# One kernel, its 1410 steps issued in another order

## The chip, the cores and the metric

The kernel runs on one core of a Trainium2 chip. The metric is the device time of one launch in microseconds (us). TensorE (PE in the profile) multiplies, VectorE (DVE), ScalarE (ACT) and GpSimd (POOL) work element by element, and SyncE (SP) issues every DMA from one queue that is worked off in order.

## The reference

The inputs are r, k, v, w of 4 batches, 8 heads, 768 tokens and 48 channels, and u of 8 heads and 48 channels. A recurrence with decay runs over the tokens, and its output goes through a feed-forward block (FFN):

```python
for t in range(S):
    cur = np.einsum('bhd,bhe->bhde', u[None] * kt, vt)
    y[:, :, t] = np.einsum('bhd,bhde->bhe', rt, state + cur)
    state = wt[:, :, :, None] * state + np.einsum('bhd,bhe->bhde', kt, vt)
...
xt = x.transpose(0, 2, 1)              # x: (4, 768, 384), the heads side by side
h = xt @ U @ V                         # mixes the tokens, rank 32
u = x + h.transpose(0, 2, 1)
ch = np.maximum(u @ w_ch1, 0.0) @ w_ch2    # 384 -> 1536 -> 384
return (u + ch).astype(np.float32)
```

## The kernel before

**Tiles.** The tokens of a batch are cut into 6 chunks of 128, so there are 24 chunks, numbered 0 to 23. Each chunk is a row of steps; a step is one small function that issues a few instructions on one engine. A step's name is a word for its work and the number of its chunk or block:

- LW, LRK, LKR, LV (SP, lines 400 to 417): loads of w, of r and k transposed, of k and r by rows, and of v. v has two buffers, so LV of a later chunk waits until an earlier chunk has been read. LRAW (L268) loads a piece of a weight, OUT (L925) stores a part of the output.
- F, R, Q (DVE, L435, L444, L449): running products of w, forward and as reciprocal. T (L172 on DVE, L170 on ACT) copies the total decay.
- PR, RP, KS, RK, RU (lines 517, 455, 459, 481, 484): elementwise products, each on POOL or DVE. DV, RED, SEL, SEL2 make a diagonal.
- AM (PE, L572) makes the scores of a chunk, CP (DVE, L576) masks them, YA and YZ (PE, L636 to L663) make the output from scores and from the state, DS (PE, L583) makes the update of the state out of k and v, ZA and ZM (L608, L617 or L619) apply it.
- KD (DVE, L560), KW and KB (SP, L377 and L383) turn k for some chunks by a transpose of blocks, a store to DRAM and four loads; KB waits for KW's data. KT and KN do it by PE. XE, XT, XN, XD do the same for the output x.
- GA, G4, SELM, GS, GSL, HP, UADD, UH, UL: the mixing by U and V. UH and UL split u into a high and a low part (ULP and UHP in the first block). UL of all three thirds must be done before the first UP of a block.

**FFN.** Each batch has 2 blocks of 384 tokens, block 0.0 to block 3.1. UP b.blk.f (PE, L867, 9 matmuls of 384 columns) makes one of 12 hidden slices, HH (ACT L874 or DVE L876) and HL (DVE L880) split it into high and low, DN b.blk.ct.part (PE, L902, 9 matmuls) adds three slices into one of three outputs, and O (DVE, L921) adds the result to x. The weights are split into high and low once: LRAW, then AB, E, SG, JN, HI, SUB per piece, w1 in 12 pieces for UP, w2 in 12 for DN. E, SG, HI, SUB, like T, HH, XE, XN, RP, KS, RK, RU, UH, UL, have an alternative engine.

**What sets the order.** Nothing is scheduled at run time. All steps of all engines stand in one list that is written out by hand as the string `ORDER`: three characters a step, two for its number and one, `how`, whose lowest bit chooses the alternative engine and whose rest is a count of warming matmuls to issue before it (`warm(s.lead)`; two counts are one bf16 matmul of 512 columns, whose result is not used). `plan` turns the string into the list:

```python
i, how = DIGITS.index(ORDER[n]) * 64 + DIGITS.index(ORDER[n + 1]), DIGITS.index(ORDER[n + 2])
...
if how % 2:
    s.eng = s.alt
s.lead = how // 2
```

An engine works its own steps in the order of the list. Between engines only the waits count that the data and the buffers demand. The list also says which buffer a step gets, since a buffer that was freed earlier is given out first.

Of the kernel before, what the change touches and what calls it, by code (L numbers as in the profile page):

```python
# [60 lines left out]

DIGITS = "0123456789ABCDEFGHIJKLMNOPQRSTUVWXYZabcdefghijklmnopqrstuvwxyz+-"
ORDER = (
    "2u02v02z02-03003502w03K03L00502+136+3113213703803A83N02y03P03913m03V00U03Q03S00003n03M04D03C03D03B03EM3W0070"
# [4 lines left out]
    "4z05B07i04+17g03l05J00u05007k05100K00a01304A05K08301807h00C04B00P01205240v05R05L05307r05M05N07l05S01411h00L0"
    "7n15O07m15Y07s00Q15P07t08608805Q00M08D08908C00O05T05U05V07u05W01505X08B07v07x07w08f07z01U07o07y05Z05a15c0871"  # L70
    "5d00y01X05e05f05h09O08E05i08A01600R08J05j05m05b01707-05k05g01A18L05l01Y16d07j15n00S00T18008W08V01905q01Z00z1"
    "0x08F08Y06e08x08+05o08g08a01B11i08h05r08d05t00+05p06C05s08508b01j08y01M01O06600-01018G05u08K08c16D08H08101k1"
    "5v01C09406E08I08i01P11l06301D06706I07+08208M00b09001E01m06J11N06406508j00d02702800e12901Q08N08Q08R08S00i0910"
    "6809308n01n00c01o00k18l06K06002A08Z10l18X08k01R10f08m01a01S12B06902000j00m00g06106206F00h00n06A06B02C09211b0"
    "8O00o15w06G01q15z01c01v08o09X09B02E01r01d01p01s08P11t02201u01e06f18s08t06H05x18p02L05+15-01f01g01w01x05y02S0"
    "9D06h01y12306i09N02g09C01z02D02G02101+02Z02F02H06L06M0CL01-12M02402508T06j16l06g02U12I02J08u02i12619502K12T0"
    "2V02W02b09q02c12N12O02P02Q08e06m06n02X16N06O06R06S06T02R02Y16U02n06P06k16o12p12a02d06X09Q06Q02j19Y06V08q09V1"
    "8z06s06W0CK08U02h09619707506t16u02e02o02f02q17607707K02k09S09Z02l02m02r06Y0980CU02s07B09a09z08-1CN07L09W09b0"
# [1066 lines left out]
```

## Time and profile before

| | |
|---|---|
| median of three runs | 427.59 us (424.26, 427.63, 427.59) |
| the profiled execution | 424.35 us, its span 422.5 us |
| PE busy | 411.8 us, 97% of the span |
| DVE busy | 279.2 us, 66% |
| ACT, POOL busy | 161.2 us, 38%; 129.4 us, 31% |
| mean granted TensorE clock | 0.998 |

The page cuts the span into 40 slices. PE has a 9 (90% or more) in almost all of them; DVE has nines in the first quarter and twos to fours at the end; the granted clock is 9 in every slice. So the shares over the whole span mix a first stretch in which four engines and the DMAs are busy with a long one in which PE is busy alone. A busy PE is not a PE at its peak, since the ends of matmuls are modelled.

### The profile page before, as it was taken

Reading aid. Unit: us, or ns where it says so; the run is one execution under the profiler, and the core shown is the slowest. Engines: PE = TensorE matmul, PEld = TensorE weight load, DVE = VectorE, ACT = ScalarE, POOL = GpSimd, SP = SyncE. Lnnn points to the kernel's source line nnn. Section 1 sums busy time; section 2 is a strip of 40 time slices with the busy share of each in tenths; the row PEclk is TensorE's granted clock in tenths of the full one; section 3 lists DMA queues with packets and bytes.
Section 4 is the critical chain, followed back from the end, with each engine's and each line's share of the span. In section 5 each row is a group of like instructions: output and inputs, shape, how many; then the busy total and the mean of one; then the engine's idle time right before and its main releaser. Section 6 shows DMA issues by size and latency. Waiting matters only on the chain. (4 is left out here: it accounts for less than half of the span.)

```text
span 422.5 us, 10580 instructions
## 1 busy us (share of the span) xinstructions
PE 411.8 (97%) x4344; PEld 384.1 (91%) x4347; DVE 279.2 (66%) x573; ACT 161.2 (38%) x434; POOL 129.4 (31%) x137
## 2 busy tenths in 40 slices
PE   8989999999999989999999999999999999999994
PEld 4876789999997989999999899999999999999994
DVE  8999899999885777974883487764664434214320
ACT  4899899885363033401122233032430113300200
POOL 5797697747351430306140222023000000100000
PEclk9999999999999999999999999999999999999999
DMA  7998836864367255446757752535532101202001
GB/s 265 330 357 307 291 89 201 279 210 127 101 156 224 76 122 137 151 119 181 181 147 169 149 139 89 148 95 119 139 83 57 38 1 50 70 20 62 2 2 59
DMA packets 64996, 58.55 MB, mean 139 GB/s; under 512 B 43184, under 2 KB 51376, under 8 KB 64944
## 3 DMA queue, kind: packets, MB, share of 16 engines
q1 hardware_dynamic: 64944, 57.83, 46.3%
q8 instruction: 35, 0.57, 0.6%
q14 instruction: 17, 0.14, 0.1%
HBM read 48.12 MB, written 9.70 MB: 137 GB/s over the span
## 5 line engine op out<-in xcount | busy, mean ns | idle before, releaser
L867 PE MATMUL f<-u,w1h 128*128 128x384 f32 x576 | 147.5, 337 | 0.4 <-DVE hl L880 0.4
L867 PEld LDWEIGHTS f<-u,w1h 128*128 128x128 f32 x576 | 103.4, 188 | 1.4 <-DVE hl L880 0.7
L902 PE MATMUL f<-hh,w2h 128*128 128x384 f32 x288 | 98.0, 340 | 0.0
L867 PE MATMUL f<-u,w1l 128*128 128x384 f32 x288 | 96.8, 336 | 0.0
L902 PE MATMUL f<-hl,w2h 128*128 128x384 f32 x288 | 96.8, 336 | 0.0
L902 PE MATMUL f<-hh,w2l 128*128 128x384 f32 x288 | 96.8, 336 | 0.0
L874 ACT ACTIVATE hh<-f 128x384 fp32r<-128x384 f32 x66 | 31.7, 489 | 143.9 <-PE f L867 143.8
L880 DVE SCALAR_TENSOR_TENSOR hl<-f,hh 128x384 fp32r<-128x384 f32 x96 | 51.5, 549 | 35.7 <-ACT hh L874 35.1
L902 PEld LDWEIGHTS f<-hh,w2h 128*128 128x128 f32 x288 | 54.1, 188 | 1.9 <-issue 1.1
L902 PEld LDWEIGHTS f<-hl,w2h 128*128 128x128 f32 x288 | 54.2, 188 | 0.1
L867 PEld LDWEIGHTS f<-u,w1l 128*128 128x128 f32 x288 | 54.1, 188 | 0.0
L902 PEld LDWEIGHTS f<-hh,w2l 128*128 128x128 f32 x288 | 54.1, 188 | 0.0
L459 POOL TENSOR_TENSOR rk<-rk,F 128x512 f32<-128x512 f32 x18 | 23.1, 1284 | 64.1 <-DMA rk<-in_rkT 31.3
L826 POOL TENSOR_TENSOR u<-xT,u 128x384 fp32r<-128x384 f32 x10 | 10.8, 1083 | 86.5 <-ACT u L820 78.0
L921 DVE TENSOR_TENSOR xT<-f,xT 128x384 f32<-128x384 f32 (+1 forms) x25 | 13.1, 535 | 33.4 <-PE f L902 28.1
L576 DVE COPY_PREDICATED A<-masks,aps 128x1024 f32<-128x1024 uint32 x24 | 31.4, 1309 | 5.3 <-PE aps L572 4.9
L435 DVE TENSOR_TENSOR_SCAN F<-w,bank 128x129 f32<-128x129 f32 x96 | 32.3, 398 | 0.6 <-POOL rk L459 0.2
L876 DVE TENSOR_SCALAR hh<-f 128x384 fp32r<-128x384 f32 x30 | 16.4, 555 | 24.2 <-PE f L867 24.0
L449 DVE TENSOR_TENSOR_SCAN Q<-w,bank 128x516 f32<-128x516 f32 x24 | 29.3, 1220 | 1.0 <-ACT Z L617 0.7
L500 POOL TENSOR_SCALAR_AFFINE_SELECT A<-dv 128x512 f32<-128x512 f32 x30 | 20.1, 676 | 20.9 <-PE y L646 10.9
L498 ACT ACTIVATE A<-ident,dv 128x128 f32<-128x128 f32 x72 | 22.7, 390 | 4.9 <-DVE dv L488 4.8
L455 POOL TENSOR_TENSOR rk<-rk,Q 128x512 f32<-128x512 f32 x15 | 19.2, 1281 | 15.6 <-DVE Q L449 13.2
(125 smaller groups left out, 541.4 us busy)
## 6 DMA issues: line engine op xcount, KB each, us to landing
rk<-in_rkT SPq DMA_DIRECT2D x24, 512.0 KB, 4.7
raw_w<-in_w SPq DMA_DIRECT2D x24, 384.0 KB, 4.7
w<-in_wT SPq DMA_DIRECT2D x30, 258.5 KB, 3.2
kr<-in_rkN SPq DMA_DIRECT2D x18, 384.0 KB, 3.9
v<-in_vN SPq DMA_DIRECT2D x24, 224.0 KB, 3.4
...
```

The lines of the kernel that those rows point to most:

```text
L435: nc.vector.tensor_tensor_scan(out=out, data0=st["row"][:, j * SEG + 1 : (j + 1) * SEG + 1][:, ::-1], data1=zeros[:, 0:SEG], initial=1.0, ...
L449: nc.vector.tensor_tensor_scan(out=flat(st["Q"]), data0=flat(st["w"]), data1=zeros, initial=1.0, op0=ALU.mult, op1=ALU.add)
L455: ENG[eng].tensor_tensor(out=rk[:, 0], in0=rk[:, 0], in1=st["Q"][:, :, 0:P], op=ALU.mult)
L459: ENG[eng].tensor_tensor(out=k, in0=k, in1=st["F"], op=ALU.mult)
L498: nc.scalar.activation(A[:, i, j], ident, AF.Copy, scale=dv[:, NP * i + j : NP * i + j + 1])
L500: nc.gpsimd.affine_select(out=A[:, i], in_=dv[:, NP * i : NP * i + NP].unsqueeze(2).broadcast_to([P, NP, P]), pattern=[[0, NP], [1, P]], c ...
L576: nc.vector.copy_predicated(by_j(st["A"]), mask8, by_j(st["aps"]))
L867: nc.tensor.matmul(ps, wt[:, f, ct, :], u[ct][:, z], start=(n == 0), stop=(n == 8))
L874: nc.scalar.activation(hh, d["ps", f], AF.Relu)
L876: nc.vector.tensor_scalar(out=hh, in0=d["ps", f], scalar1=0.0, scalar2=None, op0=ALU.max)
L880: nc.vector.scalar_tensor_tensor(out=hl, in0=d["ps", f], scalar=0.0, in1=hh.bitcast(F32), op0=ALU.max, op1=ALU.subtract)
L902: nc.tensor.matmul(d["o", ct], wt[:, 4 * ct + part, f - 3 * part, :], hid[f][z], start=(part == 0 and n == 0), stop=(part == 3 and n == 8),)
```

## The change

The string is replaced as a whole. Steps, their work and what they wait for stay the same. Read through `plan`, the two strings differ in this:

- PE has the same 350 steps, SP the same 193. DVE goes from 457 steps to 473, ACT from 286 to 277, POOL from 124 to 117. The counts of warming matmuls go from 31, 4, 11, 4, 2 (before MD 0, KT 0, DS 0, KT 3, XT 0.4) to 31, 4, 11, 2, 2 (before MD 0, KT 0, DS 0, KT 1, AM 3).
- DVE's list up to the last UL of block 0.1 that stands on DVE (UL 0.1.2 before, UL 0.1.1 after) has 128 steps before and 134 after. No longer in it: DV 4, XN 0.0, RP 5, KS 6, UHP 0.0.0, HI w1 piece 11 and 10, SUB w1 pieces 11, 6, 10, SUB w2 pieces 6, 8, HH 0.0.11, 0.0.3, 0.0.4, SG w2 pieces 5, 2, 4, 8, UH 0.1.0, 0.1.1, UL 0.1.2. New in it: T 1, 3, 8, 9, XE 3, SUB w1 piece 9, SUB w2 pieces 1, 5, 0, 2, 7, RU 6, RU 8, RK 7, HI w1 piece 8, HI w2 pieces 2, 3, 4, SG w1 piece 3, HH 0.0.10, 0.0.8, XN 1.1, RP 9, UL 0.1.0, F 10, F 11, R 11, Q 11. On PE the same 93 steps stand ahead of the first UP of block 0.1, in another order; that first UP is UP 0.1.1 before and UP 0.1.3 after. The last nine of the 93 in the new order, right ahead of it, are DN 0.0.0.0 to DN 0.0.2.0.
- SP before: OUT 0.1.1, KW 13, KB 13, OUT 0.1.0, LV 13, LKR 16; and DS 13 follows UP 1.0.0, UP 1.0.7, UP 1.0.2 on PE. After: OUT 0.0.2, LW 13, LKR 12, LV 13, KW 12, LV 11, ..., KB 12, LV 12, LW 16, KW 13, KB 13, LRK 15; LV 13 takes the buffer that YA 9 and DS 9 free. DS 13 follows UP 1.0.10, AM 13, YA 12.
- SP after, at two later loads of v: KB 16, OUT 1.0.1, LV 15; and LKR 21, OUT 1.1.2, KB 19 (four issues), LV 19. O 1.0.1 stands on DVE behind HH 1.1.4, HL 1.1.4, CP 15, and PE has DN 1.0.2.1, .2, .3, UP 1.1.11, UP 1.1.1 between UP 1.1.4 and DS 15. O 1.1.2 follows the end of DN 1.1.2.3, and PE has UP 2.0.4, .11, .10, .6, .1 between that and DS 19.

```diff
-    "2u02v02z02-03003502w03K03L00502+136+3113213703803A83N02y03P03913m03V00U03Q03S00003n03M04D03C03D03B03EM3W0070"
+    "2u02z02+12v03502w02-030031136+3213K03L02y00503m00U03n03M03703803A83V03N03913B03P03O03S03C03Q04D04C03EM0703D0"
...
-    sb2.tile([P, 64], mybir.dt.uint8, tag="gap4", name="gap4", bufs=1)
-
...
         def reduce():
-            st["dv"] = sb2.tile([P, H + 24], F32, tag="dv", name=f"dv_{g}")[:, 0:H]
+            st["dv"] = sb2.tile([P, H + 32], F32, tag="dv", name=f"dv_{g}")[:, 0:H]
...
             def copy_dv(eng):
-                st["dv"] = sb2.tile([P, H + 24], F32, tag="dv", name=f"dv_{g}")[:, 0:H]
+                st["dv"] = sb2.tile([P, H + 32], F32, tag="dv", name=f"dv_{g}")[:, 0:H]
```

The two small edits outside the string move where tiles lie in memory; the padding of dv is never read.

## Rows read from the trace of the kernel before

**Rows 1.** The page: granted clock in 40 slices.
```profile
PEclk9999999999999999999999999999999999999999
```
**Rows 2.** Stretches: length, busy PE, PEld, DVE, ACT, POOL, clock, DMA share, GB/s.
```profile
20.00:95.00 75.00, 72.80 (x1024) 63.47 (x1016) 71.48 (x136) 67.36 (x170) 56.60 (x55) 1.00 0.73 250
95.00:300.00 205.00, 203.56 (x2156) 194.28 (x2155) 145.91 (x301) 59.53 (x170) 56.26 (x57) 1.00 0.52 139
```
**Rows 3.** The timeline of DVE and of PE ahead of block 0.1: start, duration, what.
```profile
90.11 1.01 DVE L826 TENSOR_TENSOR u<-xT,u 128x384 fp32r<-128x384 f32 x2
...
93.45 0.51 PE L867 MATMUL f<-u,w1h 128*128 128x384 f32 x2
93.80 0.34 PE L867 MATMUL f<-u,w1l 128*128 128x384 f32 x1
```
**Rows 4.** Groups of DVE instructions by line: busy us, mean ns of one, idle before.
```profile
L435 DVE TENSOR_TENSOR_SCAN F<-w,bank 128x129 f32<-128x129 f32 x96 | 32.3, 398 | 0.6 <-POOL rk L459 0.2 <-DMA w<-in_wT 0.2
L449 DVE TENSOR_TENSOR_SCAN Q<-w,bank 128x516 f32<-128x516 f32 x24 | 29.3, 1220 | 1.0 <-ACT Z L617 0.7
L876 DVE TENSOR_SCALAR hh<-f 128x384 fp32r<-128x384 f32 x30 | 16.4, 555 | 24.2 <-PE f L867 24.0
L172 DVE COPY xT<-y 128x384 f32<-128x384 f32 x11 | 6.1, 551 | 3.1 <-PE y L663 3.0
L822 DVE CAST u<-xT 128x384 fp32r<-128x384 f32 x11 | 4.1, 375 | 0.1
L309 DVE SCALAR_TENSOR_TENSOR raw_w<-raw_w 128x384 uint32<-128x384 uint32 x7 | 4.1, 600 | 0.0
L459 DVE TENSOR_TENSOR rk<-rk,F 128x512 f32<-128x512 f32 x6 | 4.1, 679 | 0.0
L363 DVE TENSOR_TENSOR w2l<-cva_w,w2h 128x384 fp32r<-128x384 f32 x5 | 3.8, 752 | 0.3
L484 DVE TENSOR_TENSOR kr<-kr,u_rep 128x384 f32<-128x384 f32 x6 | 3.2, 536 | 0.0
L363 DVE TENSOR_TENSOR w1l<-cva_w,w1h 128x384 fp32r<-128x384 f32 x4 | 2.2, 542 | 0.0
L358 DVE CAST w1h<-cva_w 128x384 fp32r<-128x384 f32 x2 | 1.4, 714 | 0.0
L172 DVE COPY tots<-F 128x4 f32<-128x4 f32 x5 | 1.1, 213 | 0.0
L358 DVE CAST w2h<-cva_w 128x384 fp32r<-128x384 f32 x1 | 0.3, 350 | 0.0
```
**Rows 5.** The timeline of POOL and DVE: KS 15, and an UL beside it.
```profile
148.50 1.21 POOL L459 TENSOR_TENSOR rk<-rk,F 128x512 f32<-128x512 f32 x1
...
148.72 1.40 DVE L826 TENSOR_TENSOR u<-xT,u 128x384 fp32r<-128x384 f32 x1
```
**Rows 6.** The timeline of SP and PE around DS 13.
```profile
144.05 0.42 SPq L377 DMA_DIRECT2D turn_K<-kn  x1
148.34 2.61 SPq L383 DMA_DIRECT2D kn<-turn_K  x4
150.99 0.62 SPq L925 DMA_DIRECT2D out_dram<-xT  x1
151.66 0.43 SPq L417 DMA_DIRECT2D v<-in_vN  x1
...
153.99 0.34 PE L867 MATMUL f<-u,w1l 128*128 128x384 f32 x1
155.76 0.56 PE L583 MATMUL bank<-v,kn 128*48 128x48 f32 x16 [1.44 <-DMA v<-in_vN]
```
**Rows 7.** The timeline of PE's weight loads while warming; one matmul follows each load.
```profile
3.87 0.15 PEld L199 LDWEIGHTS <-busy 128*128 128x128 bf16 x1 [0.28 <-issue]
4.29 0.15 PEld L199 LDWEIGHTS <-busy 128*128 128x128 bf16 x1 [0.27 <-issue]
4.60 1.39 PEld L199 LDWEIGHTS <-busy 128*128 128x128 bf16 x7 [0.15 <-issue]
```

More of the change, by code (lines that the diff above doesn't have):

```diff
@@ L69 @@
[L69 to L78, printed above, removed]
@@ new lines @@
+    "3p01F03r00813R13F13W03X10000V03Y00603G03s03H00W13a43x14N03c04e03o03b03e03Z13t13y04f00900D03u10X13d03z04003+1"
+    "0G00p04F04H00A04104O03f00E01H03q14K01I11T04I03g14P04205404h03h00200314E03i03-04404301G04S04J14U44p01104m03j0"
+    "4T04j00104q00Y00Z05504k04Q04704800N04501J07f02x04g00r00s14R04r03I00F01K04G04V00B04903J04W05705907p04614X04u0"
+    "4Z05604v03k01305A04s04l11V04t00I13l07g00J15F00404w04A04B04x04i15814a00q05B15G04Y14b15H01800C04y01L15C01415K0"
+    "4z08304+14c04d00t05I05J08W04-07h07i05L07q05000H08405R05105208D07n00w01W15M05N07k00a00K07l00u05307m10L05S05Y0"
@@ new lines @@
+    "7r15O05P08607o07s07j10v05Q01M08717t00O00P08505T05U05V07x08808900M05W07u07v05X01200Q18f01507y01U05Z05d08V09q0"
+    "5e07w08B01X05i05a05b05h05j05f08J07z08C08x08A00R01Y07-05k05g05c05l08L08E11O01Z00x08Y05m08F08y00S01600y06d06C0"
+    "1A15n08g08X00T06D06e08+09000z16E05t08K08h15o05p01708005q01h08G08H08a00+08I01N05u05v01P10-08102708b06I08205r0"
+    "7+01Q01005s06608i01j01901i08c18M01k16308d02900i01B11l08j00b01R01C06401S06506701m02A18N06800k16J08k00l18Q08R0"
+    "CL00j09108n06h01v08Z00d01D18O06K06i00m01E06000e01a06F00c01n10f00n08S08T08P10o12806G16H02B06906A16101o08U15z0"
@@ new lines @@
+    "0g00h09P01x02C02009z06B09306208l05w01b01q18o05+05-02L08m09B01p01r11c19409201d05x08s08t02E08p09D06l02N11e02D1"
+    "1f01g11s01t12202311w06m02Z01y16L02105y01u12O01z01+18-02S09p06f09O02G01-12H06j02M02F02402516M08e02I02J02U0261"
+    "2P06g12T09s09u02Q02R19N02K02V16N06O02W02X12g09W02b02c16n02Y09v09y02a02n02o09Q06P02p06k12i16R06S06T06o0CK02j1"
+    "9S02d09R02e16U06V06W09t16X06y09C02f06z07806+02h06Q07919V09502k02q06v06w06Y02r02l02m07A09+16x09d02s09e18z09-0"
+    "8q08r19618u0970A009X07K06Z09T07L09809912t0Cw0CT09Y07M06-07019x06s06t06u09A0CN06a06b09Z09E06c06p0Cx09w1720710"
@@ new lines @@
+    "6q08v06r0CP09a09b07B0CS19U17317407508w0Cm0CU0Cy17C07607E09c09F0Ca09G09f09g09I0Co0CV0CW17F09J09h0A307D0CQ0Cb0"
+    "9H19K09k09r0DE09l0Cp0Cq19L0A11Cn0A207707H09i09j07N0A40CO17O07I0DF09M09m1DN0CX07P07J0Cz0C+0Cc0A50Cv0A60CM0AA0"
+    "9n0DH0Cu17G07Q09o0Cr0Cs0Ct1A71EA0A80CR0A91DM07T0D00ED0D10EF07U07R0AB0EG0Cd0AC0AD0Cf0AE0AF07V0D20DJ0AG0AK0AL0"
+    "7W0DK07Z0AH0AO0Dj0DI0Di0C-1DO0Eo07X0AI1AM07Y0AN0DL1AJ1CY0Dr0DU0Dl0CZ0AP0AQ0BI0AR17a07b0DP1Cg07c0Dq17S0An0BJ0"
+    "7d0Dn0Do0AS0Ce0Dp1Aw0D30EJ0EB07e0DV0Ch0D40Ci0DW0D50Dy0Ee0DX0D80DQ0DR0DG0EI0AT1AU0D90Ds0DS1Ao1Ax0Ap0Ay0Cj0Az0"
@@ new lines @@
+    "DT1At0Dm0DA1A+0En0A-0EH1DY0Ef0Au1DB0EC0Ab0Ac0DC0Dz0Ad0D60Av0D71Ep0Eq1AV0Dt1Aq0AY0AW0Du0D+0AX0Ah0Ai0Aj0Dc0Ar1"
+    "Dd0AZ0Aa0As0DZ0DD0BK0BL1D-0Dv0BM0EQ0HA0BN0Dw0B00EK0EE0Ae0Af0Eh0Er0Ej0Ak0Ei0IE0HB0Ag0B10Dx1ER0Al0Am0B20BO1Ek0"
+    "Hc0BP1B30HD0HI1B40El1B50B60HF0HG0B70Em1Da0B80BQ0BR0BS0EL1BT0Ck0Cl0Hl0Db1EM1EN0HJ0IY0ES0B90BC0Bg0Hf0Bh1Hh0Bi0"
+    "E00EO1BD0BE0BA0HH1EP0BF0Hi0BB0B-0Dk0BG0De1BX0E10BY1IF0BH0BZ0C00ET0E40EU0E20Eg0E50E61Es0Et1I40Eu0EV0Hd0E30EW0"
+    "Ih0IG0EX1EY0EZ0Ev0C10BU0HQ0IZ0Ea0Eb0HR0Ec0Hm0HC0HE0Ib0BV1Bd0Df0Bv0E70HT0Ew0ID0Ig1Id0BW0HS0Ie0Ex0Bw0Bx0J00Be1"
@@ new lines @@
+    "Ed0Hn1Bm0Ba0Hj1Bn0Bb0Bo0Bp0Bq0Bc0Bs0Br0Bt0Bf0Dg0Bu0Ey0Ez0Bj0Io0C20E80E+0IH0Dh0Ho0Hg0By0Bk0Bl0HK0C30Bz0I50E-0"
+    "C40HL0B+0C50HM0HN0E90C80JA0HO0HP1JV0C90CA0Hp0CB0HU0CC0F00F10Hk1Ia0CD0F20CE0C60F30C70I70IC0I90F40HV0Hs0F50Hv0"
+    "I81Ht0HX0F60IA0FA0F70F81CF0FB0JU0F91FE0FF0CG0FC1FG0FH0CH0FD1FU0Ii0Fp0CI0JB0FV1Hq1Hr1FW0Fq0CJ0JX0Fm0Fn1Fr0HW0"
+    "II0Jc0Fa0FL0Fb0Hw0Hu0IB1Fc0JY0He0Hx0IK0IN0FM0FN0IL0HY0H+0H-0HZ0If0G80JC1G90GA0Fo0Hy0Ij0Fj0IM0FR0I00Fk1IJ1Fd0"
+    "Fl0Ik1FS0I60IO0J10FT0FO0Il0Fe1FI0Ff0Im1FJ1FX0FK0JD0Hz0GC0Ir0FP1IP0FY1FQ0Ip0FZ0IS0J90IT0IQ0GD0GG0GH0I10Fs0Fg0"
@@ L103 @@
+    "KI1KZ0KL0KJ0Gz0KM0Ka0K80L00KB0K91KA0KC1KD0Kc0KN0Kb0L40L81KQ0KO0KP0KR1KS0Kd1Ke0L50KE0Kf0KF0KG0Ki0Kj0Kk05D0340"
+    "Kg0Kh0Kl04n0L914o0Ko0Kp0L10Kq0Kr0Ks0Ku0Kt0Km0Kn0LJ0Le0Lf0LK1Kv0Kw0Lg0LL0LA0Lb0LB0LC0Lc1LM0Ld0LS0LN1LT0LO0LD0"
+    "LE1Kx0LU0LF0LG0LP0LH1LI05E0LV0Ky0LQ1LW1Lk0LR0LX0LY0Lh0LZ0La0Li0Lj0Ll0Lm0Ln0Lq0Lr0Ls0Kz0Lo0Lp0Lt0Lu0Lv0Lw0Lx0"
     "Ly0Lz0L+0L-0M00M10"
```

33 lines of the change are left out of this document (5 added, 28 removed).

## The prediction, made before the changed kernel ran

> **What bounds the kernel now.** I read the page first. PE is busy for 97% of the span, but its share says little, since matmul ends are modelled; what the page does settle is that the granted clock is full in every one of the 40 slices after the very start [rows 1]. So in this execution nothing was lost to the clock later on, and TensorE's work is a fixed amount: both lists hold the same 350 PE steps. The question is then only where PE waits, and for whom.
>
> The second view is the busy time by stretch [rows 2]. From 20 to 95 us PE is busy 72.80 of 75 us, DVE 71.48, ACT 67.36. DVE has 3.5 us left, and PE 2.2. This is a stretch in which two queues are full, and a microsecond of DVE work more or less ahead of a step that PE needs can move the end. From 95 to 300 us DVE is busy 145.91 of 205 us, and PE idles 1.44 us, which is one single wait. Here DVE work is cover, and its order is worth little unless it makes some one step late. So the change is to be judged at two places: DVE's list up to the first UP of block 0.1, and that one wait.
>
> The third view is the timeline. Ahead of block 0.1 the last two ULs start at 90.11 and end at 91.12, and PE starts that block at 93.45 [rows 3]: DVE is 2.33 us early there. At the single wait the last matmul before DS 13 starts at 153.99 and the first of DS 13 at 155.76, and a load of v releases it [rows 6]. An FFN matmul takes 0.175 us from start to start (two between 93.45 and 93.80) [rows 3], so 1.77 − 0.175 = **1.6 us** are lost. The load was issued at 151.66, behind KW 13 (144.05), four KB 13 issues that had to wait for KW 13's data (148.34, 2.61 us) and one OUT (150.99): SP's queue is worked off in order.
>
> **Part 1: DVE's list up to block 0.1.** Both lists have the same 93 PE steps ahead of the first UP of that block, so PE's own work up to it is the same. DVE has 134 steps in place of 128. I price what comes and goes by the means of DVE's groups [rows 4], kind by kind, with equal kinds set off against each other:
> - SUB: two w1 pieces fewer, three w2 pieces more: −2 × 0.542 + 3 × 0.752 = +1.17.
> - HI: one w1 fewer, three w2 more: −0.714 + 3 × 0.350 = +0.34.
> - HH one fewer and UHP one fewer. UHP has no row here; it is a copy of 384 columns out of PSUM like HH, so I take 0.555: −1.11.
> - SG three fewer, −1.80; UH two fewer, −0.75; KS one fewer, −0.68.
> - T four more, +0.85; XE one more, +0.55; RK and RU three more at 0.536, +1.61.
> - F two more: 24 of them fill 32.3 us, 1.35 each, so +2.70. Q one more, +1.22. R comes and DV goes; both write a few columns as T does, at most 0.21, and cancel.
> - XN, RP, UL: one comes, one goes, 0.
>
> The sum is **+4.1 us** of DVE work ahead of PE's first UP of block 0.1. The 2.33 us by which DVE was early cover the first part, which leaves PE **1.8 us** late. The cover of the rest of this edit is that slack alone; once it is gone, the steps late next are the DN steps of block 0.0 that need SUB of w2, which stand just ahead.
>
> The bounds: if the new list fills all of DVE's idle 3.5 us [rows 2], nothing is left of 4.1 − 2.33 − 3.5, and PE could even win back the 2.2 us that it idles in the stretch: −2.2. If none of the 2.33 us can be used, because the steps that are late sit earlier in the list, it is +4.1. I take +1.8, since a queue that is busy for 71.48 of 75 us is near the full end.
>
> One row speaks against the means. One UL took 1.40 us while KS 15 ran on POOL from 148.50 for 1.21 us [rows 5], and two ULs together took 1.01 us elsewhere [rows 3]. So a step of DVE that reads two tiles can be held by POOL's, there by 1.40 − 0.5 = 0.9 us. If the three products that DVE gets (RK 7, RU 6, RU 8) are each held so, part 1 is 1.8 + 2.7 = 4.5; by the group's mean it is 1.8, and I keep that, since the mean is taken beside POOL's work as it was (56.60 of 75 us, rows 2). [...]
>
> **Part 2: the load of v before DS 13.** LV 13 moves ahead of KW 12 on SP and takes the buffer that YA 9 and DS 9 free, a whole chunk earlier than KW 13. On PE, three DN 0.1.0 steps and all of DN 0.1.1 and 0.1.2 stand between, 11 steps of 9 × 0.175 us, 17 us and more, where the load before took 4.1 us from its issue to DS 13's start [rows 6]. So this wait goes: **−1.6 us**. LV 11 now stands behind LV 13 and KW 12, and is needed by YA 11; PE has DN 0.1.0.0 to .2 and UP 0.1.10 in between, 6 us, against 4.1. KB 13 again stands right behind KW 13 and waits for its data, but behind it are only LRK 15 and other loads for later chunks. I cost that at nothing.
>
> **Part 3: what is newly tight on SP.** Two loads of v now stand late in the queue. LV 15 follows OUT 1.0.1, whose O stands behind HH, HL and CP: HL and O have no row here; at HH's 0.555, and with CP at Q's 1.22 [rows 4], O ends 3 × 0.555 + 1.22 = 2.9 us after UP 1.1.4, the OUT is issued in 0.62, and from the load's issue to DS it took 4.1 us [rows 6]: 7.6 us in all, against five PE steps of 9 × 0.175 us, 7.9 us. LV 19 follows OUT 1.1.2 and four KB issues: 0.555 + 0.62 + 2.61 + 4.1 = 7.9 us, against five steps, 7.9 us. Both just fit or just fail. The bounds are 0 and twice the old wait, 3.2; I take 0, as the two margins (0.3 and 0) are nearer to it.
>
> **Part 4: the rest.** One warming matmul goes, 0.2 us [rows 7], in a stretch where PE waits anyway; the bounds are −0.2 and, if the clock falls for it, rival 4. The moves between HH on ACT and on DVE after 95 us lie beside a DVE that is idle for 59 of 205 us [rows 2]: nothing. Tiles move in memory by the wider dv; no row shows a price for a place, and I take 0, with 0.5 either way.
>
> **The sum.** 424.35 + 1.8 − 1.6 = **424.6 us** against the profiled execution (422.5 us of span and 1.85 around it). The runs shown fall into two pairs: 424.26 and the profiled 424.35, and 427.59 and 427.63. The median is thus of the upper pair, and no trace shows what the 3.3 us are. My forecast stands in the lower pair, 0.7% below the median. With part 1 from 0 to 4.1, part 2 kept and part 3 from 0 to 1.6, its own range is 422.7 to 428.
>
> **Rivals.**
> 1. The upper pair stays: whatever cost 3.3 us in two of four executions costs it again in most. For it: it happened in half of them. Against: the wait at DS 13, the longest gap on PE, is gone. The time is 424.6 + 3.3 = 427.9.
> 2. DVE isn't late: the 3.5 us of idle time take up the new steps, and PE gets back some of its 2.2 us. For it: over its whole list ACT is relieved of nine steps and POOL of seven, so DVE may wait less for them. Against: 71.48 of 75 us. The time is 424.35 − 1.6 − 1.1 (half of 2.2) = 421.7.
> 3. POOL holds the three products, as the UL was held [rows 5]: 424.6 + 2.7 = 427.3. For it: POOL is busy for three quarters of the stretch. Against: the mean of the group, 0.536, has such cases in it.
> 4. Slower: the clock falls in the stretch from DN 0.0.0.0 to UP 0.1.3, where part 1 cuts up PE's work with waits. [...] Against it: the clock was 1.00 through 1.44 us of unbroken waiting before DS 13 [rows 1, 6]. [...]
>
> **Chances.** Forecast 0.36, rival 1 0.20, rival 2 0.25, rival 3 0.08, rival 4 0.09; for an order that comes to nothing or a wait that I did not find, 0.02. About 1% is what a measurement of this kernel can tell from no change, so the bounds are 423.3 and 431.9 us against the median. Rival 2 is faster, and of the forecast's range the part under 423.3, about 0.05: 0.30. Rival 4 and a little of rival 1 with parts 1 and 3 in full are slower: 0.10. The rest, 0.60, is no change. For 8 in 10 the range reaches down to rival 2 with 0.9 us to spare, 420.8, and up to rival 1 with half of part 3, 429.5.
>
> **What would show it.** Part 1: in the new trace DVE is busy for nearly all of 20 to 95 us, the first UP of block 0.1 starts near 95.3, and it or the DN steps ahead wait for DVE; if it starts before 93.5, part 1 is wrong. Part 2: no wait of DS 13 for v. Part 3: a wait of DS 15 or DS 19 for v, or none. Rival 4: a granted clock below 1.00 between 75 and 100 us. A run list with all times at the lower or at the upper pair's level decides rival 1. The forecast is wrong if a wait of over 3 us stands at a place that none of these names.

## The result, and the profile after

The changed kernel takes 430.25 us by the median of 20 runs (426.68 to 432.68); 20 runs of the kernel before, among them the three shown above, have a median of 426.79 (424.26 to 429.92). The ratio is **1.008, 95% interval 1.0059 to 1.010**: slower by 0.8%. The forecast was 424.6 with a range up to 429.5. Of the 20 runs of the changed kernel, the 11 with a mean granted clock of 0.985 to 0.989 took 430.1 to 432.7 us (median 430.97), and the 9 with 0.993 or more took 426.7 to 429.1 (median 428.29). Ratios here leave out an execution that is over 1.5% above the fastest of its kernel; there is one, tail20's traced one (434.72 us).

The profiled execution took 430.91 us, its span is 429.2. It is one of the 11, and that of the kernel before (424.35) is near that kernel's fastest; so the two traces differ by 6.6 us where the medians differ by 3.5. Here is the page's clock in 40 slices, which answers to [rows 1]:

```profile
PEclk9979999999999999999999999999999999999998
```

The third slice, 21 to 32 us, isn't full. The stretches show it closer, first of the changed kernel (columns as in [rows 2]), then of the kernel before:

```profile
15.00:20.00 5.00, 3.56 (x58) 2.59 (x51) 5.00 (x6) 4.45 (x13) 3.31 (x4) 0.99 0.88 272
20.00:26.60 6.60, 6.60 (x97) 5.66 (x95) 6.23 (x15) 4.65 (x14) 4.98 (x6) 0.50 0.64 218
26.70:30.00 3.30, 3.15 (x72) 2.66 (x65) 2.35 (x4) 2.26 (x7) 1.78 (x3) 1.00 0.88 286
20.00:95.00 75.00, 71.42 (x1050) 60.87 (x1046) 70.29 (x133) 65.75 (x168) 49.52 (x49) 0.96 0.72 239
95.00:300.00 205.00, 204.04 (x2157) 194.04 (x2156) 154.67 (x318) 66.14 (x183) 57.56 (x57) 1.00 0.52 142
```
```profile
15.00:20.00 5.00, 4.90 (x114) 3.99 (x112) 4.80 (x11) 4.97 (x17) 3.73 (x5) 1.00 0.90 294
20.00:26.60 6.60, 6.11 (x140) 5.17 (x134) 6.57 (x13) 6.57 (x17) 6.34 (x8) 1.00 0.99 337
```

Two things stand there. From 15 to 20 us PE is busy 3.56 of 5 us, before 4.90. And then the granted clock is 0.50 from 20 to 26.6 us: PE is "busy" all the time but issues 97 matmuls in place of 140. From 20 to 95 us DVE is busy 70.29 us, less than before.

**Where the time went, step by step.** Two kinds of step were not named so far, both on PE: MD multiplies what PR made by u, for the diagonal, and VM spreads the weight V. Both lists hold the same PE steps ahead of some of their places, and there the starts can be compared. The table gives them for the kernel before (us from the start of the span, first matmul of the step in the timeline) and, for the others, how much later they are. DN 0.0.0.2 stands seven PE steps ahead of block 0.1's first UP, which in the changed kernel is as late as it, 6.77 us; DN 1.0.2.0 is behind DS 13.

```
             MD 4   HP 0.1.0  DN 0.0.0.2  HP 1.0.2  DN 1.0.2.0  DN 3.1.2.3
before      24.56     51.11      82.53     144.61     191.14     415.40
after       +4.58     +5.73      +6.77      +7.33      +6.24      +6.63
head20      +0.68     +0.39      +2.25      +2.85      +1.76      +1.65
tail20      +6.22     +7.76      +7.73      +8.28     +10.22     +10.23
nohold      +2.37     +2.99      +3.88      +4.46      +3.35      +4.07
warm        +2.73     +3.89      +4.56      +5.12      +4.02      +3.92
ks2_first   +1.56     +2.49      +3.60      +4.17      +3.07      +3.98
hl3         +1.96     +2.35      +2.67      +3.68      +2.55      +3.47
jn11        +1.09     +1.07      +1.88      +2.52      +1.40      +1.81
mended      +1.17     +1.42      +2.20      +3.15      +2.06      +2.07
allfix      +2.24     +1.95      +2.44      +3.39      +2.28      +3.64
hold_in     +1.29     +1.49      +1.51      +1.60      +2.09      +2.24
lv13        +0.69     +1.21      +1.20      +1.19      -0.31      -0.32
head118     +0.35     +0.52      +0.50      +0.56      -0.52      -0.30
late_OUT    +0.67     +0.96      +0.95      +1.03      +2.19      +2.23
```

The row of the changed kernel reads: 4.6 us are lost by MD 4, 1.15 more by HP 0.1.0, 1.0 by DN 0.0.0.2, 0.6 by HP 1.0.2; then 1.1 are won at DS 13, and 0.4 lost again. (The early step KT 0 starts up to 0.8 us later than in the kernel before, in traces of whatever kernel. The weight loads of the warming matmuls ahead of it start 0.43 us apart at first and 0.20 apart from 4.6 us on in the kernel before, from 6.3 us on in the changed one, at a granted clock of 1.00 in both; so a few tenths in a row mean nothing. In the changed kernel it is 0.6 us, so 4.0 of the 4.6 us belong to the order.)

**The first place, 15 to 20 us.** Timelines of the changed kernel: DVE (PR 2, JN V0, KS 2, CP 1), POOL (PR 3, RP 2) and PE (DS 1, KT 2, MD 3, AM 2, DS 2):

```profile
15.28 1.27 DVE L515 TENSOR_TENSOR kr<-rk 128x256 f32<-128x256 f32 x2
16.47 0.88 DVE L312 SCALAR_TENSOR_TENSOR cva_V<-cva_V,raw_V 128x192 uint32<-128x192 uint32 x1
17.27 1.67 DVE L457 TENSOR_TENSOR rk<-rk,F 128x512 f32<-128x512 f32 x1
18.86 1.30 DVE L574 COPY_PREDICATED A<-masks,aps 128x1024 f32<-128x1024 uint32 x1
```
```profile
15.36 1.78 POOL L515 TENSOR_TENSOR kr<-rk 128x256 f32<-128x256 f32 x2
17.10 1.29 POOL L453 TENSOR_TENSOR rk<-rk,Q 128x512 f32<-128x512 f32 x1
```
```profile
15.81 0.56 PE L581 MATMUL bank<-v,kn 128*48 128x48 f32 x16 [0.66 <-ACT kn L170]
...
19.04 0.63 PE L549 MATMUL trk<-ident,rk 128*128 128x128 f32 x4 [0.78 <-issue]
...
20.83 1.87 PE L522 MATMUL trd<-u_diag,kr 128*128 128x2 f32 x8
22.63 1.56 PE L570 MATMUL aps<-rk 48*64 48x128 f32 x32
...
27.01 0.56 PE L581 MATMUL bank<-v,kn 128*48 128x48 f32 x16
```

and of the kernel before, DVE (PR 2, CP 1, KS 2), POOL (RP 2) and PE (KT 2):

```profile
14.80 0.74 DVE L517 TENSOR_TENSOR kr<-rk 128x256 f32<-128x256 f32 x2
15.46 1.31 DVE L576 COPY_PREDICATED A<-masks,aps 128x1024 f32<-128x1024 uint32 x1
16.66 0.72 DVE L459 TENSOR_TENSOR rk<-rk,F 128x512 f32<-128x512 f32 x1
```
```profile
15.62 1.20 POOL L455 TENSOR_TENSOR rk<-rk,Q 128x512 f32<-128x512 f32 x1 [1.59 <-DVE kr L517]
```
```profile
17.63 0.66 PE L551 MATMUL trk<-ident,rk 128*128 128x128 f32 x4
```

KS 2 comes to its turn at 17.27, 0.17 us after RP 2 began on POOL, and ends at 18.94, 0.55 us after RP 2's end at 18.39; it takes 1.67 us in place of 0.72. PR 2 takes 1.27 in place of 0.74 beside PR 3. Of what KT 2 needs KS 2 ends last, and KT 2 starts 0.1 us after it, whatever "issue" says. In the kernel before it is CP 1 that runs beside RP 2, and that takes 1.31 us, as it takes 1.30 in the changed kernel with POOL idle. CP 1 reads its scores from PSUM, KS 2 both its tiles from SBUF. The other gap on PE, the 0.66 us ahead of DS 1, is a wait for KN 1 on ACT, which took 0.52 us, in the kernel before 0.51.

### The profile page after: what moved, and what is told of

Same layout as the page of the kernel before. It is cut to its first block, busy times and chain, and to the rows that moved or that the text cites. A ratio compares the mean times of both kernels' runs of the same rounds, so it can differ in the third digit from the quotient of the medians.

```text
span 429.2 us, 10594 instructions
## 1 busy us (share of the span) xinstructions
PE 416.1 (97%) x4343; PEld 386.3 (90%) x4346; DVE 289.6 (67%) x589; ACT 161.0 (38%) x425; POOL 123.2 (29%) x130
## 4 chain that ended last, share of the span: by engine, by line
PE 78%; DVE 9%; POOL 3%; DMA 3%; issue 3%; ACT 2%; DVEq 0%; POOLq 0%; ACTq 0%
PE f L900 30%; PE f L865 29%; PE aps L570 3%; PE y L634 2%; PE bank L581 2%; DMA raw_w<-in_w 2%; PE y L644 2%; PE idle L199 2%; PE y L657 2%; DVE cva_w L312 2%; DVE F L433 1%; DMA rk<-in_rkT 1%; PE trd L522 1%; POOL raw_w L295 1%; POOL w1l L361 1%
## 5 line engine op out<-in xcount | busy, mean ns | idle before, releaser
L872 ACT ACTIVATE hh<-f 128x384 fp32r<-128x384 f32 x57 | 27.7, 491 | 120.4 <-PE f L865 120.2
L874 DVE TENSOR_SCALAR hh<-f 128x384 fp32r<-128x384 f32 x39 | 21.5, 553 | 23.9 <-PE f L865 23.8
L824 POOL TENSOR_TENSOR u<-xT,u 128x384 fp32r<-128x384 f32 x7 | 7.5, 1079 | 84.9 <-ACT u L818 84.9
L496 ACT ACTIVATE A<-ident,dv 128x128 f32<-128x128 f32 x76 | 24.0, 391 | 13.5 <-DVE dv L486 9.9
L453 POOL TENSOR_TENSOR rk<-rk,Q 128x512 f32<-128x512 f32 x18 | 22.8, 1265 | 21.4 <-issue 13.5
L457 POOL TENSOR_TENSOR rk<-rk,F 128x512 f32<-128x512 f32 x15 | 18.5, 1233 | 18.7 <-DVE F L433 8.1
```

The lines of the kernel that those rows point to most:

```text
L453: ENG[eng].tensor_tensor(out=rk[:, 0], in0=rk[:, 0], in1=st["Q"][:, :, 0:P], op=ALU.mult)
L457: ENG[eng].tensor_tensor(out=k, in0=k, in1=st["F"], op=ALU.mult)
L496: nc.scalar.activation(A[:, i, j], ident, AF.Copy, scale=dv[:, NP * i + j : NP * i + j + 1])
L872: nc.scalar.activation(hh, d["ps", f], AF.Relu)
L874: nc.vector.tensor_scalar(out=hh, in0=d["ps", f], scalar1=0.0, scalar2=None, op0=ALU.max)
```

## The experiments

Orders are given as an engine's list of steps; w1/2 is piece 2 of w1.

**1. head20, tail20: which half of the list.** The cut is behind the 20th PE step, where both lists have done the same PE steps.

```diff
-steps: all in the order after
+head20: order before up to MD 4, then order after
+tail20: order after up to MD 4, then order before
```

> The first 20 PE steps (to MD 4, 24.56 us before, 29.13 us after) with all that stands among them come from the order before, the rest is the order after. Theory E (early): after's loss is made here. In its trace KT 2 starts at 19.04 in place of 17.63 us, since KS 2, PR 2 and JN V0 on DVE take 1.67, 1.27 and 0.88 us beside POOL's steps in place of 0.71, 0.74 and 0.35, and the granted clock is at the lower level from 19.86 to 26.68 us; 4.6 of the 6.6 us are there at MD 4. Then this kernel wins about 4 us on the changed one: 426 us by the median, 425.5 to 427, the granted clock at 1.00 after 5 us. Theory D: the list of DVE up to block 0.1 is what costs, and DVE is behind anyway; an earlier MD 4 only makes PE wait longer for DVE, at HP 0.1.0 and DN 0.0.0.0. Then 429 to 430 us, with waits of PE for DVE of 3 us or more between 40 and 100 us.

> The other half: the first 20 PE steps from the order after, the rest from the order before. Theory E: the loss is in the first 20 steps and stays: 430 to 431.5 us, KT 2 at 19.0 us or so, a granted clock at the lower level between 19 and 27 us in the profiled execution or in about half of the runs. Theory D: the first steps cost little at the end: within 1 us of the kernel before, 426 to 428 us.

head20 took 427.34 us, ratio 1.0031 (0.9997 to 1.0064); tail20 430.12, 1.0059 (1.0025 to 1.0092). So most of the loss stands in the first 20 steps, though the intervals of the two halves overlap and head20 did not come down to the expected 425.5 to 427. Its row shows what is left: 1.86 us between HP 0.1.0 and DN 0.0.0.2. tail20's trace shows something besides (PE behind the wait of DS 13, and the stretches around it):

```profile
162.27 0.34 PE L865 MATMUL f<-u,w1l 128*128 128x384 f32 x1
164.48 0.56 PE L581 MATMUL bank<-v,kn 128*48 128x48 f32 x16 [1.87 <-DMA v<-in_vN]
```
```profile
160.00:165.00 5.00, 3.13 (x36) 2.79 (x35) 2.21 (x7) 1.19 (x3) 0.00 (x0) 1.00 0.82 215
165.00:170.00 5.00, 5.00 (x76) 4.55 (x75) 3.71 (x6) 2.34 (x8) 1.64 (x2) 0.66 0.51 137
```

The old wait for v is 1.87 us here in place of 1.44, and the clock is low behind it (0.66 over 5 us), which the profiled execution of the kernel before did not show. It is the slowest of the ten runs, and the row stands for that one.

**2. warm: the clock by itself.**

```diff
-DS 1 (no warming), KT 2 (none)
+DS 1 behind 3 warming matmuls, KT 2 behind 3.5
```

> The order after with warming matmuls put into the two early waits and nothing else changed: 3 of 512 columns before DS 1 (it waited 0.66 us), 3.5 before KT 2 (0.78 us). KT 2 can't come earlier by it. Theory E with the clock as a part of its own: what PE does before 19.86 us decides whether the clock falls; filled up, it stays at 1.00 and the 6.8 us at the lower level go. Its steps from MD 3 to YZ 1 took 6.2 us there in place of about 4: 428 us, 427.5 to 428.7, that is 2 us under the changed kernel and still 1 to 2 above the one before. If the fall does not depend on these waits (a rival): 430 to 431 us, the clock low in the same place. If the warming matmuls themselves delay KT 2: up to 0.5 us on top.

428.06 us, 1.0040 (1.0010 to 1.0069); 9 of 10 runs have a mean clock of 0.996 or more. The stretches:

```profile
15.00:20.00 5.00, 4.59 (x62) 2.96 (x55) 5.00 (x6) 4.65 (x16) 3.80 (x4) 1.00 0.76 259
20.00:25.00 5.00, 4.42 (x111) 3.60 (x109) 4.97 (x13) 4.74 (x13) 2.96 (x4) 1.00 0.78 269
```

KT 2 came no earlier (19.53 us; KS 2 again took 1.67), but PE was kept at work in the gap, and the clock stayed at 1.00. In the four kernels with this filling (warm, hl3, jn11, allfix) none of 46 runs has a mean clock under 0.99, where the changed kernel has 11 of 20. So, as expected, about half of the 0.8% was the clock: 0.4% by the ratios, whose intervals overlap, and about the same by the changed kernel's own runs, where 11 of 20 are slower than the other 9 by 2.7 us in the median.

**3. nohold, hold_in, ks2_first: POOL beside DVE.**

```diff
 nohold, on the order after
-POOL: E w1/2, PR 3, RP 2     DVE: Q 2, PR 2, JN V0, KS 2, CP 1
+POOL: RP 2, PR 3             DVE: JN V0, Q 2, PR 2, CP 1, KS 2     ACT: E w1/2 ahead of its SG
 hold_in, on the order before
-POOL: RP 2, PR 3             ACT: E w1/2, SG w1/2, XE 0
+POOL: E w1/2, PR 3, RP 2     ACT: XE 0, SG w1/2
 ks2_first, on the order after
-DVE: PR 2, JN V0, KS 2
+DVE: PR 2, KS 2, JN V0
```

> The order after with PE's and SP's order untouched; four steps of other engines moved: E of w1 piece 2 from POOL to ACT ahead of its SG, JN V0 on DVE ahead of Q 2, CP 1 on DVE ahead of KS 2, PR 3 on POOL behind RP 2. So no long step of POOL lies beside PR 2, JN V0 and KS 2. Theory E, that it is POOL's steps that hold DVE's there: the three take 0.4 to 0.8 us each, KS 2 ends by 17.8 in place of 18.94 us, KT 2 starts 1 us or more earlier, and if the clock fell because of PE's waits there, it stays up: 426.5 to 428.5 us. Theory D: KS 2 comes earlier but the time stays within 1 us of the changed kernel, 429.3 to 431 us. If the steps are long again without POOL beside them, holding by POOL is wrong.

> The kernel before with the arrangement on POOL that the changed kernel has at 14 to 18 us, and nothing else of the change: E of w1 piece 2 goes from ACT to POOL (its SG two places later on ACT), and PR 3 goes ahead of RP 2 on POOL. DVE's and PE's orders are untouched. Theory E: POOL now runs from 14.2 to 18.3 us without a gap, so PR 2 and KS 2 on DVE are held (1.2 and 1.6 us in place of 0.74 and 0.71), KS 2 ends at 18.9 in place of 17.37, KT 2 starts at 19.0 in place of 17.63 us, and the loss stays to the end: +1.4 us, 427.5 to 428.5 by the median, and 430 where the clock falls after the wait, which it may do in some of the runs. Rival: what is lost there is taken back in PE's waits at MD 3 and KT 3 (0.5 us before) and the time is within 0.5 us of the kernel before.

> The changed kernel with one step moved: KS 2 ahead of JN V0 on DVE. KT 2 on PE waits for KS 2 and for nothing else. In the changed kernel KS 2 comes to its turn at 17.27 us, just after RP 2 has begun on POOL (17.10 to 18.39), and ends at 18.94. Theory E: one place earlier it starts ahead of RP 2, so RP 2 is the one that is held, KS 2 ends by 17.8 and takes under 1.2 us, KT 2 has no wait after VM V1 (18.3 in place of 19.04 us) and 0.8 us are won: 429.5 us by the median where the clock still falls as often, down to 427.5 where it does not. Rival: KS 2 is as long as before (1.6 us) in another place, so it isn't RP 2 that holds it; and 430 to 431 us.

nohold took 429.55 us, 1.0064 (1.0032 to 1.0096). The three steps took 0.73, 0.36 and 0.69 us, so the holding is gone, but the edit brought waits of its own: JN V0, now ahead of Q 2, waited 1.77 us for ACT, and DS 1 waited 1.47 us for KN 1. It shows the cause of the long steps and nothing of the time. Its trace also shows what the clock costs: from MD 3 to DS 2 PE needs 3.48 us here, at a clock of 1.00, and 6.18 in the changed kernel.

```profile
20.66 1.05 PE L522 MATMUL trd<-u_diag,kr 128*128 128x2 f32 x8
...
24.14 0.56 PE L581 MATMUL bank<-v,kn 128*48 128x48 f32 x16
```

hold_in did nothing: 427.25 us, 0.9991 (0.9964 to 1.0018). Its timelines (DVE, POOL) say why:

```profile
17.33 0.76 DVE L459 TENSOR_TENSOR rk<-rk,F 128x512 f32<-128x512 f32 x1
```
```profile
17.49 1.64 POOL L455 TENSOR_TENSOR rk<-rk,Q 128x512 f32<-128x512 f32 x1
```

KS 2 was first by 0.16 us, and now RP 2 is the long one (1.64 in place of 1.20 us), as KS 2 was in the changed kernel, where RP 2 was first by 0.17 us. My expectation had the order of arrival wrong.

ks2_first took 431.90 us, 1.0130 (1.0093 to 1.0167), the slowest of all. KS 2 took 1.10 us and KT 2 had no wait, as expected; but JN V0 was late in its place, VM V1 waited 0.65 us for it, and 4 of 5 runs have a mean clock of 0.991 to 0.995. The gap had only moved by one step. The traced one is the fifth run (428.05 us), and its mean clock is 1.00, in spite of two gaps of that length (DS 1, VM V1):

```profile
15.77 0.56 PE L581 MATMUL bank<-v,kn 128*48 128x48 f32 x16 [0.67 <-ACT kn L170]
...
17.97 0.85 PE L332 MATMUL vm<-cva_V,ident 128*32 128x192 f32 x12 [0.65 <-DVE cva_V L312]
```

So behind two such gaps the clock fell in the changed kernel's trace (0.50 from 20 to 26.6 us) and not in this one. Where it fell in the other four runs no trace shows.

**4. hl3, jn11, and the two together (allfix, mended): DVE between 40 and 100 us.** In the changed kernel JN w1/11 stands ahead of the ULs that HP 0.1.0 and the first UP need, and it takes 1.37 us beside SUB w1/11 on POOL (0.54 in jn11); HL 0.0.3 stands behind SG w2/0, which waits for an E on POOL. Timelines of the changed kernel, DVE, POOL and PE at the one place, and DVE and PE at the other:

```profile
54.94 1.37 DVE L312 SCALAR_TENSOR_TENSOR cva_w<-cva_w,raw_w 128x384 uint32<-128x384 uint32 x1
56.23 1.01 DVE L824 TENSOR_TENSOR u<-hp,u 128x384 fp32r<-128x384 f32 x2
...
83.43 0.57 DVE L307 SCALAR_TENSOR_TENSOR raw_w<-raw_w 128x384 uint32<-128x384 uint32 x1 [1.18 <-POOL raw_w L295]
...
87.21 0.54 DVE L878 SCALAR_TENSOR_TENSOR hl<-f,hh 128x384 fp32r<-128x384 f32 x1
```
```profile
54.60 1.29 POOL L361 TENSOR_TENSOR w1l<-cva_w,w1h 128x384 fp32r<-128x384 f32 x1 [2.84 <-ACT w1h L354]
```
```profile
56.84 0.44 PE L806 MATMUL hp<-Vst,gs 96*128 96x384 f32 x1 [0.86 <-DVE u L824]
...
87.81 0.45 PE L900 MATMUL f<-hl,w2h 128*128 128x384 f32 x1 [0.35 <-DVE hl L878]
```

```diff
 hl3, on warm
-DVE: SUB w2/0, JN w2/2, HI w2/2, UADD 0.1.2, HL 0.0.3
+DVE: SUB w2/0, HL 0.0.3, JN w2/2, HI w2/2, UADD 0.1.2
 jn11, on warm
-DVE: RP 7, JN w1/11, ULP 0.0.1, ULP 0.0.2
+DVE: RP 7, ULP 0.0.1, ULP 0.0.2, JN w1/11
 allfix = warm + both;  mended = the order after + both + KS 2 first + 3 warming matmuls before DS 1 alone
```

> The kernel with the warming matmuls (428.06 us) with one more step moved: HL 0.0.3 directly behind SUB of w2 piece 0 on DVE, three places earlier. DN 0.0.0.1 waits for it (0.35 us before its second matmul, and it took 2.35 us in place of 1.72). Theory, that part 1's loss is the place of single steps behind SG of w2 piece 0, which waits for POOL's E until 80 to 83 us, and not a sum of all of DVE's work: DN 0.0.0.1 loses its wait and 0.5 to 0.8 us are won, 427.4 us. Rival, part 1 as it was priced: DVE is full, another step is late in its place (SUB of w2 piece 2 at DN 0.0.0.2), and nothing is won, 428 us.

> The kernel with the warming matmuls (428.06 us) with one more step moved: JN of w1 piece 11 on DVE behind ULP 0.0.2 in place of ahead of ULP 0.0.1. In the changed kernel it took 1.37 us beside SUB of w1 piece 11 on POOL (54.60 to 55.89) in place of 0.55, and HP 0.1.0 waited 0.86 us for the two ULs behind it. Theory E: the wait at HP 0.1.0 gets shorter by 0.5 to 1.3 us (by the lower bound if ULP 0.0.1 is now held in JN's place), 427 to 427.6 us. Rival: UP 0.0.1, which needs what JN w1 piece 11 leads to, waits instead: 428 us.

> The changed kernel with 3 warming matmuls before DS 1 and 3.5 before KT 2, HL 0.0.3 behind SUB of w2 piece 0, and JN of w1 piece 11 behind ULP 0.0.2. Alone the two moves won 0.6 and 1.3 us on the kernel with the warming matmuls. If they add up: 428.06 less 1.9 = 426.2 us, within 1 us of the kernel before. If DVE's list as a whole is the limit, one gain eats the other: 426.8 us or more.

> The changed kernel with the moves of KS 2, HL 0.0.3 and JN of w1 piece 11 together and 3 warming matmuls before DS 1 (none before KT 2, which shouldn't wait any more). If the losses of the change are these three places and the clock, they add up: 430.25 less 0.8 (KS 2), 0.6 (HL), 0.9 (JN) and 2.2 (clock, what the warming matmuls won) = 425.7 us, under the kernel before by 1. If DVE as a whole is the limit up to block 0.1, the moves only shift the waits: 427.5 us or more, with PE's waits for DVE between 40 and 100 us as long in sum as in the changed kernel.

jn11 took 426.79 us, 1.0011 (0.9988 to 1.0034); the wait at HP 0.1.0 is gone, and between MD 4 and HP 0.1.0 nothing is lost, where warm lost 1.16. hl3 took 427.49, 1.0020 (0.9995 to 1.0045); between HP 0.1.0 and DN 0.0.0.2 it loses 0.32, where warm lost 0.67. Against warm neither gain is clear of the noise by the time alone, but the traces repeat: the five traces with the changed order from the start and without the move of JN (the changed kernel, nohold, warm, ks2_first, hl3) all show the wait of 0.86 us at HP 0.1.0, and the three with the move none (nor does head20, which has the old start); DN 0.0.0.1 takes 1.56 us in the three with the move of HL, and 1.97 to 2.41 in the six others that have the changed order there. allfix took 427.32, and its ratio is **1.0001 (0.9977 to 1.0026)**: with four edits the loss against the kernel before is gone, as far as that interval tells. Whether the two gains add up the intervals can't tell; by the ratios the two win 0.4% on warm together, and 0.3 and 0.2 alone. mended went to 431.06, 1.0100 (1.0065 to 1.0135): without the warming matmuls before KT 2 it has the gap before VM V1 (0.63 us) and a mean clock of 0.994 or less in 5 of 6 runs; its one profiled execution has 0.997 and took 425.9.

hl3's trace (DVE's JN V0 and KS 2, POOL's PR 3) also shows how narrow the race at the first place is:

```profile
15.43 0.35 DVE L312 SCALAR_TENSOR_TENSOR cva_V<-cva_V,raw_V 128x192 uint32<-128x192 uint32 x1
15.70 0.68 DVE L457 TENSOR_TENSOR rk<-rk,F 128x512 f32<-128x512 f32 x1
```
```profile
15.90 1.76 POOL L515 TENSOR_TENSOR kr<-rk 128x256 f32<-128x256 f32 x2 [1.13 <-PE bank L581]
```

The same list as in warm up to here, but PR 3 began late (1.13 us of idle time ahead of it; in jn11 0.62, in mended 0.45 and in ks2_first 0.38, put down to the load of rk), and DVE got through ahead of it. So the same three steps of DVE are held in some executions and not in others: KS 2 took 1.67 us in the changed kernel, warm and allfix, 1.21 in jn11 and 0.68 here.

**5. lv13, late_OUT, lv13_warm, head118: the wait for v.**

```diff
 SP, order before
-LW 16, OUT 0.1.1, KW 13, KB 13, OUT 0.1.0, LV 13, LKR 16, OUT 0.1.2
+lv13:     LW 16, LV 13, OUT 0.1.1, KW 13, KB 13, OUT 0.1.0, LKR 16, OUT 0.1.2
+late_OUT: LW 16, OUT 0.1.1, KW 13, KB 13, OUT 0.1.0, LKR 16, OUT 0.1.2, LV 13
 lv13_warm = lv13 + 1.5 warming matmuls before AM 3 and 2 before AM 4
 head118   = order before up to DN 0.1.0.0, then order after
```

> The kernel before with one step moved on SP: LV 13 stands ahead of OUT 0.1.1 and KW 13 in place of behind OUT 0.1.0. Its buffer is free since YA 11, before 130 us. The prediction's part 2: the wait of 1.44 us before DS 13 goes, and with it 1.6 us: 425.2 us by the median against 426.8, 0.996 times. Rival: the next load is late in its place (KW 13 and KB 13 are issued 0.4 us later, and DS 13 or KN 13's users wait), 426.5 to 427.5.

> The kernel before with LV 13 moved the other way on SP, behind LKR 16 and OUT 0.1.2, so that it is issued 1.4 us later. If the wait before DS 13 costs its own length alone: it goes from 1.4 to 2.8 us, and the time rises by 1.4 us, 428.5 us. If the granted clock falls behind that wait in a part of the runs, as it did in the other half of the change (from 165.78 to 169.19 us behind a wait of 1.87 us), then with the longer wait it falls in more of them: 2.5 to 4 us over the kernel before, 429.6 to 431 us, and most runs show a mean clock of 0.99 or below.

> The version with LV 13 earlier (424.57 us) with 1.5 warming matmuls before AM 3 and 2 before AM 4, where it waited 0.7 and 1.0 us. Its runs have a mean clock of 0.993 to 0.999; if some of that is lost behind these two waits, it is won back: 424.0 to 424.4 us, and fewer runs above 425. If the clock does not fall there: the same 424.6 us; if the warming matmuls end after the wait, up to 0.3 us more.

> The order before up to its 118th PE step (DN 0.1.0.0, 120 us), then the order after for all that is left; so of the change there is only what comes after block 0.1's UPs, and DS 13 does not wait for v. Theory E, and part 1 of the prediction too: all that the change lost is ahead of this place (7.3 us of PE's time at HP 1.0.2, 6.6 at the end), so this kernel is 1.0 to 1.6 us faster than the kernel before: 425.2 to 425.8 by the median, 422.7 to 423.3 where the clock is full from the start. Rival: the list after 120 us is worse too, as LV 15 and LV 19 are newly tight (a wait of 1 us at DS 15 or DS 19): 427 to 428.

**lv13 took 424.57 us, 0.9927 (0.9900 to 0.9954)**, the fastest with lv13_warm, 424.30, 0.9950 (0.992 to 0.998); one step moved, and both kernels are beaten. head118 took 425.61, 0.9957 (0.9926 to 0.9988): what the change does behind 120 us is a gain, so the loss is made ahead of that. late_OUT took 428.76, 1.0039 (1.0013 to 1.0065). DS 13 in lv13 and in late_OUT:

```profile
155.18 0.34 PE L867 MATMUL f<-u,w1l 128*128 128x384 f32 x1
155.45 0.56 PE L583 MATMUL bank<-v,kn 128*48 128x48 f32 x16
```
```profile
155.02 0.34 PE L867 MATMUL f<-u,w1l 128*128 128x384 f32 x1
157.95 0.56 PE L583 MATMUL bank<-v,kn 128*48 128x48 f32 x16 [2.59 <-DMA v<-in_vN]
```

lv13's trace wins 1.5 us at this place, as priced; the interval of the time says 2 to 4. Part of the rest is that the wait isn't always 1.44 us: in nowarm3 (below) it was 1.8, in hold_in 1.9, in tail20 1.87 with the clock low behind it. With late_OUT's 2.59 us the mean clock is 0.997 (0.998 in the kernel before's trace), so the length of the wait alone doesn't decide. Another part shows in the clock: of the 33 runs of the kernel before beside lv13, 17 have a mean clock under 0.995, and the other 16 have a median of 426.60 us; of lv13's 10 runs one is under 0.995, and of late_OUT's six. So with the wait go falls of the clock as well, and against the 16 lv13 wins 2.0 of its 3.1 us. Where the clock falls in those 17 runs no trace shows, so this stays argued; lv13_warm's 2.1 us would need less of it. The warming before AM 3 and AM 4 made no difference that the intervals show. In hold_in the clock was low just behind these steps, after a gap of 0.59 us in AM 3:

```profile
25.00:27.00 2.00, 1.65 (x32) 1.57 (x36) 1.68 (x4) 1.76 (x3) 1.95 (x3) 1.00 1.07 360
27.00:30.40 3.40, 3.40 (x70) 2.94 (x64) 2.56 (x4) 2.43 (x8) 2.55 (x4) 0.50 0.94 351
```

**6. tiles, nowarm3: what was priced at nothing.**

```diff
 tiles, order before
-dv: H + 24 columns, gap4
+dv: H + 32 columns, no gap4
 nowarm3, order before
-KT 3 behind 2 warming matmuls
+KT 3 behind none
```

> The kernel before with the two small edits outside the string alone: dv with 32 spare columns in place of 24, no gap4. The order is that of before. Both theories: a tile's place in memory is worth nothing, 426.8 us, within 0.5 us of the kernel before, and the trace shows the same waits. Rival: the place of a tile costs; then this kernel carries 1 us or more of the changed kernel's 3.5, and DVE's steps on dv or on what lies behind it are longer than before.

> The kernel before without the two warming matmuls before KT 3; PE waits there for about 0.8 us in all. As the prediction priced them: no change, within 0.5 us of the kernel before. If what PE does in its early waits decides whether the clock falls: the mean clock is 0.99 or below in half of the runs or more and the time rises by 1.5 us or more, 428.5 us or above.

tiles 426.36 us, 0.9988 (0.9955 to 1.0022): nothing. nowarm3 426.08, 0.9971 (0.9948 to 0.9993): no loss, and 2 of 10 runs with a clock under 0.995; in its trace KT 3 waits 0.85 us and the mean clock is 0.998. The two warming matmuls before KT 3 that the change took away were not the cause.

## Why the prediction was wrong

**The step that failed** is in its second paragraph: "So the change is to be judged at two places: DVE's list up to the first UP of block 0.1, and that one wait." I had drawn the two places from rows that begin at 20 us and from where the old kernel was tight, but the string is replaced from its first step on, and the new order has its own tight places. 4.6 of the 6.6 us in the trace are lost by MD 4 (4.0 without the late KT 0), where I had costed one warming matmul: 0.8 us are the gap before KT 2, and 2.7 the clock behind it. To find it I would have had to put both lists side by side on POOL and DVE from 10 us on and to ask, of each DVE step that reads two tiles from SBUF, what POOL does at that time.

**The base of the sum** was wrong too. I added to the traced execution, 424.35 us, and the median of 20 runs is 426.79: 2.4 of the 5.65 us by which the forecast missed are that choice. The change itself was forecast at +0.2 and measured at +3.5. (And the sum's own upper end, 424.35 + 4.1 − 1.6 + 1.6, is 428.45, not 428.)

**Part 1**, +1.8: the size came out near, by luck. In head20, whose first steps are those of before, PE loses 1.86 us between HP 0.1.0 and DN 0.0.0.2 (1.04 in the changed kernel, which comes late to it, and 0.67 in warm), and its first UP of block 0.1 starts at 95.70 us, where 95.3 was forecast. The reason was mostly another: not a sum of work on a full queue, since DVE is busy for 70.29 of 75 us, less than before, and idle for 1.18 us ahead of SG w2/0. The two F and the Q that made up 3.9 of my 4.1 us stand behind UL 0.1.0, when PE has its DN steps, and cost 0.25 us at UP 0.1.7. Single steps stood in the wrong place: HL 0.0.3 for one, as hl3 shows.

**Part 2**, −1.6: right. DS 13 has no wait in the changed kernel, its trace wins 1.1 us there, and lv13 alone is faster by 2 to 4 us. **Part 3**, 0: right for the changed kernel, there is no wait of DS 15 or DS 19 for v; how tight it is show nohold and ks2_first, where DS 19 waits 0.44 and 0.46 us. **Part 4**: right in both prices, as far as tiles and nowarm3 test them.

**The rivals.** Rival 1 rested on two pairs of times that were no pairs: of 20 runs 12 lie between the two. I had four numbers and read a structure into them. What spreads the runs is at least in part the clock: of the 122 runs of the kernel before that stand beside the experiments, 46 have a mean clock under 0.995 and a median of 427.9 us, the other 76 one of 426.2. Rival 3 (POOL holds DVE's products) was right on other steps; of the three that I named only RU 8 was held (1.35 us, where such a step has a median of 0.55). Those that mattered were KS 2 (1.67 us, in nohold 0.69), PR 2 (1.27 and 0.73) and JN V0 (0.88 and 0.36), and JN w1/11 (1.37, in jn11 0.54). Rival 4 (the clock falls where waits cut up PE's work) was right too, at 20 us in place of 75 to 100. No row of the kernel before shows what a lower clock costs; in the changed kernel YA 1, YZ 1, MD 3 and AM 2 took 6.18 us, nearly all at 0.50, in nohold at 1.00 they took 3.48, so it was 2.7 us. I argued against it with one wait of 1.44 us at full clock. That was one execution; behind 1.87 us in tail20 the clock was low (0.66 over 5 us).

By the ratios the warming matmuls give back 0.4 of the 0.8%, JN w1/11 0.3 and HL 0.0.3 0.2, each with about 0.25% either way. The change's own gain at DS 13 is in allfix too, which is nevertheless no faster than the kernel before; so about as much as that gain, 0.4% or more, is still lost elsewhere. In allfix's trace 1.6 us of it are lost by MD 4 (beyond KT 0's 0.6), where KS 2 is again 1.67 us long, 0.95 between DN 0.0.0.2 and HP 1.0.2, and 1.4 behind DN 1.0.2.0; there PE waits 0.94 us for an HL at 218.79, where the changed kernel has 0.42 and the kernel before no wait. No run tests these last places.
